# Input gradient of a convolution stem: the second batch with three products for all three leaves, each in its own PSUM tile

## The chip, the core and the metric

The kernel runs on one core of a Trainium2 chip. The metric is the device time of one execution in microseconds (us). The engines are TensorE (PE, matmuls, fed by weight loads, PEld), VectorE (DVE), ScalarE (ACT), GpSimd (POOL) and SyncE (SP, which issues nearly all transfers here). The program lists the operations once, each with its inputs, outputs and an estimated duration, and a planner writes out the order of every engine by hand before anything is emitted.

## The reference

A strided one-dimensional convolution (31 taps, stride 2, 256 channels in and out, two batches of 16000 steps), a normalization over time, and a gelu; the outputs are the forward result and the gradients of all four inputs in bf16.

```
B, T, D, K = 2, 16000, 256, 31
s = 2
L = (T - K) // s + 1                         # 7985
h = sum over i of x[:, i:i + s*L:s, :] @ w[i]
mu, var = mean and variance of h over l
h = (h - mu) / sqrt(var + 1e-5) * gn_gamma + gn_beta
out = gelu(h)                                # tanh form
out, grads of (x, w, gn_gamma, gn_beta) for grad_out
```

## The kernel before

**Stages.** F0 and F1 are the forward of batches 0 and 1 (to about 422 us), G0 and G1 the input gradient (about 422 to 862 us), W the weight gradient (to the end). The gelu of batch 0 and its derivative run beside F1, those of batch 1 beside the first chunks of the input gradient.

**A convolution by fewer products.** The 31 taps are split three times in two. The first two levels use three products in place of four: branches B, A, C (`ORDER`) for the first, leaves B, A, C for the second. For each pair the weights of the branch and leaf are differences or originals, held in `W2`. At the third level a leaf can be computed plainly (`g_leaf`, 16 matmuls) or by three products again: `g_three_b` (4 matmuls with weight differences from `W2D`, and a copy with the sign changed into the second half of the PSUM tile) and `g_three_ac` (8 matmuls with the sums from `GU`). The sums of the moving data come from VectorE: `first` makes the branch's planes (`GS`) from the element tile `ET`, `second` those of leaves A and C (`GL`), `third` the third level's (`GU`, `GUO`).

**The input gradient now.** `input_grad` goes over batches `b`, chunks `c` (four a batch), half chunks `pr` and, innermost, branches `br`. A unit is one half chunk and branch. It takes two of the four PSUM tiles (`slots4`): leaf B goes into `px` by three products, `g_seed` turns that and the kept results of branch B (`GRB`, fp32) into the starting values of leaves A and C on VectorE or ScalarE, and in the next unit `last(A)` and `last(C)` accumulate these leaves on top, and `g_evac` copies them into `HO`. In batch 0, A and C are plain; in batch 1 (`GO`) leaf A has three products, whose difference product `g_outer` lies in the other tile and is joined through `GTS` (fp32). After branch C's leaf C one transfer of 1 MB per half chunk writes `out_1`.

**What feeds it.** For each chunk `e_load` loads the stored gelu derivative (into `EG`) and h (into `EH`), `e_comp` scales and adds them into the gradient of the convolution's output and spreads it into one of two tiles `ET`; `dn_turn` transposes it and stores it to DRAM (`dn_d`). From there `d2_piece`, seven pieces a batch, computes the differences for the weight gradient (line 1338) and stores them to `d2_d`, from which `d_tile` of the weight gradient loads its tiles. The pieces share one source tile `DT`.

**The order.** `Plan.add` records an operation and what it must wait for; `due` times are worked back from the end over durations, with `lead` shifting a kind of operation; `listing` runs a list schedule. TensorE may take an operation up to `look` = 14 ahead of its written order. Operations on transfers get part of their slack added:

```
room = max(0.0, due[s] + slip - r) * 0.3
if ops[s]["dma"] is not None:
    r += min(self.pads[0 if o["dma"] is None else 1], room)
```

Lines the text names: 1168 matmuls of the input gradient, 602 of the forward, 1428 of the weight gradient; 682 and 686 joins of 1024 elements, 689 and 693 of 512; 697 copies out of PSUM, 1195 the sign copy; 1127 sums; 557 weight differences; 1073, 1075 and 1077 scaling and adding, 1087 spreading; 1338 the pieces; 1042 the last statistic of a batch; 1394, 1488, 1496, 1520 and 1566 work of the weight gradient on VectorE; 974 products of the gelu part; 1457 the emission of weight gradients; 424 and 429 transfers.

## Time and profile before

| | |
|---|---|
| time, median of 3 runs | 1189.31 us (1188.89 to 1189.55) |
| span of the profiled execution | 1190.2 us |
| TensorE busy | 1148.1 us, 96% |
| VectorE busy | 1044.0 us, 88% |
| ScalarE busy | 578.9 us, 49% |
| GpSimd busy | 24.9 us, 2% |
| transfers | 255.17 MB, mean 214 GB/s |
| granted TensorE clock | 0.997 |

Busy times are unions over an engine's instructions; the mean of a group counts each instruction from its start to its end, and neighbours overlap a little. A row of the waits gives what waited, for whom, the total, the number and the longest. A row by windows gives the window, its length, and for each engine the busy time and the number of instructions, then the granted clock, the busy share of the transfer engines and GB/s. The chain of waits is followed back from the last instruction.

### The profile page before, as it was taken

The page shows a single profiled execution, that of the slowest core. Times are in us where ns is not written, and L with a number is a line of the kernel's source. Part 1 is how long each engine was busy: PE and PEld are TensorE (multiplying, and loading weights), DVE is VectorE, ACT ScalarE, POOL GpSimd, SP SyncE. Part 2 cuts the span into 40 slices and gives each one's busy share as a digit, 9 for nine tenths or more (in the row PEclk, how much of TensorE's full clock was granted, in tenths as well). Part 3 has the DMA queues.
Part 4 walks back from the last instruction along what each step waited for, and adds up shares of the span by engine and source line. Part 5 has one row for each costly group of instructions (what it writes and reads, how often), then busy time and mean ns, then how long its engine had stood idle before and what let it go on. Part 6 is the DMA issues. An engine that isn't in the chain of part 4 may idle for free.

```text
span 1190.2 us, 19351 instructions
## 1 busy us (share of the span) xinstructions
PE 1148.1 (96%) x7755; PEld 764.2 (64%) x7812; DVE 1044.0 (88%) x1351; ACT 578.9 (49%) x879; POOL 24.9 (2%) x67
## 2 busy tenths in 40 slices
PE   5999999999999999999999999999998999989998
PEld 4888899776776964444444444444487766656685
DVE  7997798899999989999889897788888999679995
ACT  1244454678875578978785776433222212211200
POOL 0000000000000000101000000000000000000000
PEclk9999999999999999999999999999999999989999
DMA  9464838889894799766738998697898727997674
GB/s 212 67 140 103 184 92 194 197 186 196 195 231 109 252 318 268 214 221 161 236 123 260 287 321 286 167 312 251 281 258 270 236 91 229 327 306 237 226 215 116
DMA packets 334084, 255.17 MB, mean 214 GB/s; under 512 B 187484, under 2 KB 312666, under 8 KB 325722
## 3 DMA queue, kind: packets, MB, share of 16 engines
q1 hardware_dynamic: 333802, 253.93, 76.2%
q8 instruction: 61, 1.00, 0.3%
q14 instruction: 29, 0.24, 0.1%
q0 software_dynamic: 192, 0.00, 0.0%
HBM read 118.95 MB, written 89.62 MB: 175 GB/s over the span
## 4 chain that ended last, share of the span: by engine, by line
PE 72%; DVE 11%; DMA 7%; ACT 4%; issue 3%; SPq 2%; POOL 0%; DVEq 0%; ACTq 0%; POOLq 0%
PE ps L602 30%; PE ps L1168 24%; PE ps L1428 17%; DVE arena L1394 2%; DMA arena<-dnd 2%; DMA arena<-d2d 2%; DMA d2d<-arena 1%; DVE arena L1338 1%; DMA arena<-in_x_dram 1%; SPq L429 1%; ACT arena L717 1%; DVE arena L557 1%; DVE arena L1488 1%; DVE arena L1496 1%; SPq L424 1%
## 5 line engine op out<-in xcount | busy, mean ns | idle before, releaser
L1168 PE MATMUL ps<-arena 128*128 128x512 bf16 (+1 forms) x1974 | 429.2, 376 | 5.3 <-DVE ps L682 2.0
L602 PE MATMUL ps<-arena 128*128 128x256 bf16 (+4 forms) x3460 | 407.2, 280 | 21.6 <-DVE arena L557 7.5
L602 PEld LDWEIGHTS <-arena 128*128 128x128 bf16 x3460 | 337.1, 98 | 91.8 <-issue 8.8
L1168 PEld LDWEIGHTS <-arena 128*128 128x128 bf16 x2016 | 197.4, 98 | 235.8 <-issue 4.9
L1428 PE MATMUL ps<-arena 128*128 128x256 bf16 (+1 forms) x2321 | 312.6, 297 | 11.7 <-DVE arena L1488 5.4
L1428 PEld LDWEIGHTS <-arena 128*128 128x128 bf16 x2336 | 229.7, 98 | 94.6 <-issue 6.2
L697 ACT ACTIVATE arena<-ps 128x1024 f32<-128x1024 f32 (+1 forms) x143 | 145.9, 1021 | 250.4 <-PE ps L1428 95.0
L567 DVE TENSOR_TENSOR arena<-arena 128x1088 bf16<-128x1088 bf16 (+3 forms) x211 | 175.2, 865 | 15.4 <-PE ps L602 14.4
L974 DVE TENSOR_TENSOR arena<-arena 128x1024 bf16<-128x1024 bf16 x160 | 106.7, 683 | 10.1 <-ACT arena L966 6.4
L1127 DVE TENSOR_TENSOR arena<-arena 128x516 bf16<-128x516 bf16 (+3 forms) x176 | 83.7, 507 | 14.1 <-PE ps L1168 13.3
L1394 DVE TENSOR_TENSOR arena<-arena 128x4096 bf16<-128x4096 bf16 x38 | 86.1, 2282 | 3.6 <-DMA arena<-in_x_dram 1.8
L682 DVE TENSOR_TENSOR ps<-ps,arena 128x1024 f32<-128x1024 f32 x60 | 73.3, 1224 | 12.9 <-PE ps L1428 8.1
L1338 DVE TENSOR_TENSOR arena<-arena 128x768 bf16<-128x768 bf16 (+3 forms) x112 | 65.9, 636 | 10.1 <-DMA arena<-dnd 6.8
L717 ACT ACTIVATE arena<-ps 128x512 bf16<-128x512 f32 (+1 forms) x64 | 36.9, 580 | 59.7 <-PE ps L602 59.7
L682 DVE TENSOR_TENSOR ps<-arena,ps 128x1024 f32<-128x1024 f32 x44 | 53.8, 1223 | 9.5 <-PE ps L1168 5.3
L1512 ACT COPY ps<-ps 128x256 f32<-128x256 f32 x54 | 19.3, 358 | 81.1 <-PE ps L1428 79.9
L1496 DVE TENSOR_TENSOR arena<-arena 128x1024 bf16<-128x1024 bf16 x76 | 49.0, 682 | 8.2 <-DMA arena<-d2d 6.7
L1566 DVE TENSOR_TENSOR arena<-arena 128x2304 bf16<-128x2304 bf16 x36 | 47.8, 1349 | 4.1 <-DMA arena<-d2d 4.1
L1195 ACT ACTIVATE ps<-ps 128x512 f32<-128x512 f32 x48 | 27.9, 582 | 47.6 <-PE ps L1168 47.3
L557 DVE TENSOR_TENSOR arena<-arena 128x2048 bf16<-128x2048 bf16 (+1 forms) x52 | 50.5, 990 | 0.0
L672 ACT ACTIVATE arena<-ps 128x512 f32<-128x512 f32 x56 | 29.0, 601 | 38.9 <-PE ps L602 32.9
L638 ACT ACTIVATE ps<-ps 128x256 f32<-128x256 f32 x75 | 27.5, 367 | 41.0 <-PE ps L602 39.8
(79 smaller groups left out, 672.1 us busy)
## 6 DMA issues: line engine op xcount, KB each, us to landing
arena<-in_x_dram SPq DMA_DIRECT2D x40, 1024.0 KB, 9.4
arena<-d2d SPq DMA_DIRECT2D x16, 1216.0 KB, 10.5
out_dram<-arena SPq DMA_DIRECT2D x14, 1024.0 KB, 5.5
d2d<-arena SPq DMA_DIRECT2D x30, 384.0 KB, 7.3
arena<-dnd SPq DMA_DIRECT2D x10, 960.0 KB, 6.6
vl<-arena SPq DMA_DIRECT2D x36, 256.0 KB, 3.3
arena<-vl SPq DMA_DIRECT2D x9, 1024.0 KB, 5.6
hd<-arena SPq DMA_DIRECT2D x8, 1024.0 KB, 5.2
```

The costliest lines, as they stand in the source:

```text
L557: add("DVE", dve(n), [o], [a, b], lambda: nc.vector.tensor_tensor(out=o, in0=a, in1=b, op=ALU.subtract))
L567: lambda: nc.vector.tensor_tensor(out=o, in0=a, in1=b, op=ALU.add))
L602: yield nc.tensor.matmul(ps[:, dh, cs], lhsT=wt, rhs=mv, start=s0, stop=False, skip_group_check=True)
L682: add("DVE", dve(1024, 1), [out], [a, b], lambda: nc.vector.tensor_tensor(out=out, in0=a, in1=b, op=op))
L697: lambda: nc.scalar.activation(out=out, in_=ps, func=ACT.Copy, scale=scale))
L974: add("DVE", dve(1024), [o], [a, b_], lambda: V.tensor_tensor(out=o, in0=a, in1=b_, op=op))
L1127: lambda: nc.vector.tensor_tensor(out=o, in0=a, in1=b, op=ALU.add))
L1168: yield nc.tensor.matmul(ps[:, e, 0:wide], lhsT=lt, rhs=mv, start=s0, stop=False, skip_group_check=True)
L1338: lambda: nc.vector.tensor_tensor(out=out, in0=a, in1=b_, op=ALU.subtract))
L1394: add("DVE", dve(4096), [o], [a, b], lambda: nc.vector.tensor_tensor(out=o, in0=a, in1=b, op=ALU.add))
L1428: yield nc.tensor.matmul(ps[:, s, c0:c1], lhsT=lt, rhs=mv, start=s0, stop=False, skip_group_check=True)
L1496: add("DVE", dve(1024), [d4[:, j]], [d], lambda j=j, o=o, st_=st_: nc.vector.tensor_tensor(out=d4[:, j], in0=d[:, o:o + 3 * st_ + 1:st_, : ...
```

## The change

The units of batch 1 and of chunk (0, 3), named by `GV`, are computed by `split`: leaves B, A and C each by three products in a PSUM tile of its own, handed out by a list `free`. Leaf B is copied to SBUF in bf16 (`VT`), joined there with `GRB` (now bf16), and the finished leaves are joined with that in bf16 on the way to `HO`: by a copy and a join in place for all of branch B and for leaf A, by one join out of PSUM for leaf C of branches A and C (`GE`). The other units (`plain`) start leaves A and C from leaf B alone and join with `GRB` at the end. `W2D` holds nine differences in place of three and three in `W2DO`. The loop over branches lies outside that over the half chunks; `out_1` is written by `g_store` after each branch A and C, 512 KB in runs of 1024 bytes. There is one `ET` and one `GS` in place of two; the spreading is a step of its own, `e_spread`, placed after the first half of branch C of the chunk before. In the forward, the kept results `RB` and `TS` are bf16. The table `lead` is replaced, and some addresses of the weight gradient move.

```
-    RB = sb(146944, 2, 1024, dt=FP32)
+    RB = sb(146944, 2, 1024)
...
-    ET = [sb(o, 2, 4, 2, EM) for o in (165376, 182016)]
-    GS = [sb(o, 2, 2, 2, 2, EM) for o in (190336, 94336)]
+    EG, ET = sb(86016, 2, 2, 4, HM), sb(165376, 2, 4, 2, EM)
+    GS = sb(181888, 2, 2, 2, 2, EM)
...
-                ve(t, RB[:, j], t, ALU.add if br == A else ALU.subtract)
+                add("DVE", dve(1024), [t], [RB[:, j], t], lambda t=t, j=j: nc.vector.tensor_tensor(
+                    out=t, in0=RB[:, j], in1=t, op=ALU.add if br == A else ALU.subtract))
...
+    def g_join(o, a, b, op, rate):
+        add("DVE", dve(1024, rate), [o], [a, b], lambda: nc.vector.tensor_tensor(out=o, in0=a, in1=b, op=op))
+
+    def g_store(b, c, pr, br, ho):
+        n0 = 512 * c + 256 * pr
+        r = P if c < 3 or pr == 0 else 104
+        dst = bass.AP(tensor=out_1.tensor, offset=out_1.offset + (b * T + 8 * n0 + 2 * (br == C_)) * C,
+                      ap=[[16 * C, r], [4 * C, 4], [1, 2 * C]])
+        load(dst, ho[0:r].rearrange("p e k f -> p (e k) f"), r * 4096, 1024, "POOL", slack=60.0)
+
+    GV = {(b, c) for b in range(NB) for c in range(NCK) if (b, c) >= (0, 3)}
+    GE = {(b, c, pr, br, lf) ... if br == B_ or lf == A}
...
+        def plain(b, c, pr, br, o, sums):
...
+            g_three_b(px, br, B_, pl[B_], o)
+            if pr == 0:
+                second(A)
+            step()
+            g_three_ac(px, br, B_, gu[B_], o)
+            if pr == 0:
+                second(C_)
+            step()
+            keep(flat2(pt), flat2(px), -1.0)
...
+                g_leaf(ps, br, lf, pl[lf], o, False)
...
+                    g_join(ho[:, :, j, :], ps[:], rb, ALU.subtract if br == A else ALU.add, 1)
...
+        def split(b, c, pr, br, o, sums):
...
+            x = free.pop(0)
+            if pr == 0:
+                third(B_)
+            g_three_b(ring[x], br, B_, pl[B_], o)
+            if pr == 0:
+                second(A)
+            step()
+            a = free.pop(0)
+            g_three_b(ring[a], br, A, pl[A], o)
+            if pr == 0:
+                third(A)
+                second(C_)
+            g_three_ac(ring[x], br, B_, gu[B_], o)
+            vx = vtile()
+            keep(vx, ring[x][:])
+            free.append(x)
+            step()
...
+                g_join(ts[C_], vx, GRB[:, pr, 1], ALU.subtract if br == A else ALU.add, 2)
+                g_join(vx, vx, GRB[:, pr, 0], ALU.add if br == A else ALU.subtract, 2)
+            k = free.pop(0)
+            g_three_b(ring[k], br, C_, pl[C_], o)
+            if pr == 0:
+                third(C_)
...
+            last(A)
+            rest.append(lambda: last(C_))
...
+                for br in ORDER:
+                    sums = g_sums(br, k)
+                    k += 1
+                    sums[0]()
+                    for pr in range(2):
+                        (split if (b, c) in GV else plain)(b, c, pr, br, P * pr, sums)
...
+        if (br, pr) == (C_, 0) and nxt < (2, 0):
+            e_spread(*nxt)
```

473 lines of the change are left out of this document (244 added, 229 removed).

## The prediction

> **What bounds the kernel now.** I read the page first, then the busy time by stage, then the waits of TensorE in the input gradient, and last the chain of waits around the end of that stage. The profiled execution has this span; it stands 0.9 us above the median of the runs (1189.31), so I work on 1190.2 and take 0.9 off at the end.
>
> ```profile
> span 1190.2 us, 19351 instructions
> ```
>
> The busy times of three stretches: the end of the forward of the second batch, the input gradient (about 422 to 862 us), and the weight gradient.
>
> ```profile
> core 0: us, PE busy (x) PEld busy (x) DVE busy (x) ACT busy (x) POOL busy (x), PEclk, DMA share, GB/s
> 300.00:422.00 122.00, 120.28 (x977) 95.18 (x976) 118.33 (x166) 82.73 (x142) 3.81 (x11) 1.00 0.81 195
> 422.00:862.00 440.00, 434.78 (x2041) 203.55 (x2080) 385.42 (x608) 287.83 (x356) 16.86 (x43) 1.00 0.81 247
> 862.00:1190.00 328.00, 313.02 (x2324) 229.81 (x2337) 277.04 (x240) 54.95 (x89) 0.53 (x1) 0.99 0.74 229
> ```
>
> The reader is to see two nearly full engines. In the input gradient TensorE is busy 434.8 of 440 us; VectorE 385.4, which is 88%; ScalarE 287.8, which is 65%. What TensorE waits for in the whole stage is next to nothing; these are all its waits, in total, number and longest:
>
> ```profile
> PE ps L1168 <- DVE ps L682: 2.0, 3, 1.4
> PE ps L1168 <- ACT arena L697: 0.5, 1, 0.5
> PE ps L1168 <- ACT arena L717: 0.5, 1, 0.5
> ```
>
> So the stage is bound by TensorE, and matmuls taken away shorten it as long as nothing else comes to the front. One thing stands close behind. In the chain of waits for 780 to 870 us no matmul of the input gradient carries the time from 783 us to the weight gradient: the differences of the output gradient (d2_piece of batch 1) do, from a load of dnd through VectorE to a store into d2d and a load out of it. Where it leaves TensorE, its last steps, and TensorE at the same place:
>
> ```profile
> 779.75 3.20 PE ps L1168 x14
> ...
> 836.06 4.41 DMA arena<-dnd
> ...
> 848.79 10.15 DMA d2d<-arena
> 859.02 5.68 DMA arena<-d2d
> 864.74 5.29 PE ps L1428 x47
> ```
>
> ```profile
> 862.40 0.60 PE L1428 MATMUL ps<-arena 128*128 128x256 bf16 x4
> 864.74 31.60 PE L1428 MATMUL ps<-arena 128*128 128x256 bf16 x288 [1.74 <-DMA arena<-d2d]
> ```
>
> TensorE ended the input gradient at about 862.4, did four matmuls of batch 0, and then stood 1.74 us until the d2 tile of batch 1 was there. The two ends meet within about 2.3 us: whatever shortens the matmuls of the input gradient meets the d2 chain at once.
>
> **The matmuls.** The code fixes their number: three products a leaf cost 4 + 8 matmuls, a plain leaf 16. A unit (a half chunk and a branch) now has 12 + 16 + 16 = 44 in batch 0 and 4 + 4 + 8 + 8 + 16 = 40 in batch 1; a split unit has 3 x 12 = 36. All 24 units of batch 1 lose 4 and the 6 units of chunk (0, 3) lose 8: 96 + 48 = 144 matmuls out of 2016. The price of one comes from the busy times of line 1168 alone, by weight loads, since some matmul records are missing:
>
> ```profile
> 650.00:758.00 108.00, 107.47 (x496) 49.41 (x505) 1.00 0.93 281
> ```
>
> 108 us by 505 is 0.214 us, so the change removes 144 x 0.214 = 30.8 us. That this is saved at all hangs on what follows.
>
> **VectorE in the input gradient.** The prices, from the groups by shape:
>
> ```profile
> L974 DVE TENSOR_TENSOR arena<-arena 128x1024 bf16<-128x1024 bf16 x160 | 106.7, 683 | 10.1 <-ACT arena L966 6.4 <-ACT arena L968 2.6
> ...
> L682 DVE TENSOR_TENSOR ps<-ps,arena 128x1024 f32<-128x1024 f32 x60 | 73.3, 1224 | 12.9 <-PE ps L1428 8.1 <-ACT arena L697 4.8
> ...
> L1127 DVE TENSOR_TENSOR arena<-arena 128x514 bf16<-128x514 bf16 x68 | 28.2, 423 | 1.3 <-PE ps L1168 1.3
> ...
> L1457 DVE TENSOR_TENSOR arena<-ps,arena 128x1024 bf16<-128x1024 f32 x15 | 18.3, 1218 | 6.8 <-PE ps L1428 6.8
> ...
> L689 DVE TENSOR_TENSOR arena<-ps,arena 128x512 f32<-128x512 f32 x16 | 10.9, 683 | 2.8 <-PE ps L1168 1.4 <-ACT arena L697 1.2
> ```
>
> and, since an instruction's busy time overlaps its neighbour's in a dense run,
>
> ```profile
> 741.96 1.23 DVE L682 TENSOR_TENSOR ps<-arena,ps 128x1024 f32<-128x1024 f32 x1
> 743.09 1.22 DVE L1077 TENSOR_TENSOR arena<-arena 128x2048 bf16<-128x2048 bf16 x1
> ```
>
> the second starts 1.13 us after the first, so I take 0.09 off each. Added: the sums third for leaf C in 12 (chunk, branch) pairs and for A and C in three more, 18 pairs of 2 x 0.33 us = 11.9 us. The joins before, for a half chunk of batch 1: five of 1024 in fp32 on PSUM (1.13) and four of 512 (0.60), 8.05 us; eight halves are 64.4 us, and chunk (0, 3) has eight of 1.13, 9.0 us. After, for a half chunk: branch B two joins all in bf16, which I price by the 1024-wide bf16 instruction of line 974 (0.60), branches A and C each three of these and one from PSUM, priced by line 1457 (1.13): 1.2 + 2 x 2.93 = 7.06 us, ten halves 70.6. So the joins get 2.8 us cheaper. The weight differences for leaf C are three more instructions like these:
>
> ```profile
> L557 DVE TENSOR_TENSOR arena<-arena 128x2048 bf16<-128x2048 bf16 x30 | 36.0, 1215 | 0.0
> ```
>
> 3.4 us. Together +12.5: VectorE needs 398 us in a stage that shall last 440 - 30.8 = 409, which is 97%. The nearest row for such a density is the stretch 300 to 422 above: VectorE 118.3 of 122 (97%), TensorE idle 1.7 us, or 1.4%. For 409 us that is 5.8, against the 3.0 of waits above that the stage loses today: +2.8 us, with 0 and +12 as the ends (nothing lost; twice that row's share). In the plain units left in batch 0 the seeds on VectorE become joins from PSUM at the same price, so nothing changes there.
>
> **ScalarE and the PSUM ring.**
>
> ```profile
> L697 ACT ACTIVATE arena<-ps 128x1024 f32<-128x1024 f32 (+1 forms) x143 | 145.9, 1021 | 250.4 <-PE ps L1428 95.0
> ...
> L1195 ACT ACTIVATE ps<-ps 128x512 f32<-128x512 f32 x48 | 27.9, 582 | 47.6 <-PE ps L1168 47.3
> ```
>
> Per split half chunk ScalarE has nine copies of 0.58 and seven of 1.02, 12.4 us, against 9.0 now (five of about 0.58 and six of 1.02); in a plain half chunk branches A and C each have one of 1.02 less. That is +26 in batch 1, +7 in (0, 3), -12 in the plain chunks: 309 of 409 us, 76%. The sign copy behind each first product is covered by the 12 matmuls between it and its use (2.6 us), which a 0.58 copy behind one 1.02 copy fits into; a freed PSUM tile is written again 24 matmuls (5.1 us) after its last one. Nothing from me for this; if the cover is gone, 0.2 us for each of 30 units, 6 us. The output stores become 32 half-size transfers in place of 16, in shorter runs, all in SyncE's one queue, where the d2 stores also stand; that belongs to the next part.
>
> **The d2 chain.** It is the step that moves against the change. Today the element tile ET is doubled, so the gradient of chunk (1, 3) was computed while chunk (1, 1) still ran. With one ET and the copies in e_spread, the chain is: branch B of (1, 1) has read ET; e_spread (1, 2); then the gradient buffer EG is free for the load of (1, 3); scaling, adds, transposes, dnd, seven pieces. SyncE's queue and ScalarE today:
>
> ```profile
> 721.99 0.51 SPq L424 DMA_DIRECT2D arena<-dyd  x1
> ...
> 744.84 5.51 SPq L429 DMA_TRANSPOSE arena<-arena  x2
> ...
> 757.65 0.35 SPq L424 DMA_DIRECT2D arena<-dnd  x1
> ...
> 825.03 0.33 SPq L424 DMA_DIRECT2D arena<-dnd  x1
> ...
> 836.06 0.33 SPq L424 DMA_DIRECT2D arena<-dnd  x1
> ```
>
> ```profile
> 729.98 4.25 ACT L1075 ACTIVATE arena<-arena,stats 128x1024 bf16<-128x1024 bf16 x4
> ...
> 745.47 0.82 ACT L1087 COPY arena<-arena 128x768 bf16<-128x768 bf16 x1
> ...
> 747.10 3.34 ACT L1087 COPY arena<-arena 128x768 bf16<-128x768 bf16 x5
> ```
>
> With G ending at 862.4 - 30.8 - 1 + 2.8 = 833 and chunks of 216 x 0.214 = 46.2 us, chunk (1, 1) starts at 694.4. Branch B's second half has read ET after 40 matmuls, at 703; e_spread takes 5 us of copies (745.5 to 750.4 above) and some POOL copies, to 710; the load of dyd was followed by its first scaling 8.0 us later, four of those (4.25) and the last add make about 14 us, to 724; from the transposes to the first dnd load are 12.8 us (744.84 to 757.65), to 737; from there to the first matmul of batch 1 today's trace takes 864.74 - 757.65 = 107.1 us: 844. The pieces start 13.0 us apart on average (757.65 to 836.06, six steps), at best 11.0 (825.03 to 836.06), and the planner stretches DMA-bound steps where it sees slack; at the best pace the chain gains 6 x 2 + 2 = 14 us: 830. So TensorE would find its data between 830 and 844, when it is ready at 833 + 0.6. I take 840, nearer the traced pace because VectorE, which each piece needs for some 4 us, is fuller: a gap of about 7 us where there are 2.3 today, +4.7.
>
> Such a gap costs more than itself. The weight gradient has one already, 5.07 us up to 1044.7; the granted clock after it:
>
> ```profile
> 1040.00:1044.00 4.00, 0.00 (x0) 0.00 (x0) 4.00 (x5) 0.23 (x1) 0.00 (x0) 0.91 1.04 331
> ...
> 1048.00:1050.00 2.00, 2.00 (x12) 1.39 (x11) 0.00 (x0) 0.61 (x2) 0.00 (x0) 0.50 1.09 346
> 1050.00:1052.00 2.00, 2.00 (x19) 1.79 (x18) 0.00 (x0) 1.07 (x3) 0.00 (x0) 0.97 1.10 349
> ```
>
> The clock stood at 0.50 for about 6 us after that gap. Those 3 lost us are all that the mean of 0.99 over 862 to 1190 leaves room for, so the gap of 1.74 cost nothing of the kind; a 7 us gap costs 3 more. The Trainium skill (TensorE: Matmul & The Clock Gate, Part 1: The HAM clock gate) says that the array falls to half clock after an idle window of about 3.4 us; the trace agrees, with 1.74 us below it and 5.07 above. Without the gate the sum would end at 1165, with it at 1168.
>
> **The rest.** The forward: the 20 joins of this group go from fp32 to bf16, from 1.13 to 0.60 us, 10.6 us of VectorE; but what TensorE waits for most there once it has started is ScalarE:
>
> ```profile
> L682 DVE TENSOR_TENSOR arena<-arena 128x1024 f32<-128x1024 f32 x20 | 24.1, 1221 | 7.5 <-ACT arena L672 6.4 <-ACT arena L697 1.0
> ```
>
> ```profile
> PE ps L602 <- ACT arena L717: 6.8, 9, 1.4
> ```
>
> With the new order I take -1, between -5 and +4. The start of batch 1's first chunk hangs on the statistics of the second batch, which ended here:
>
> ```profile
> L1042 DVE SCALAR_TENSOR_TENSOR stats<-small x2: 149/155/161, 399.7 to 629.4; 128x2 f32<-128x2 f32 x2
> ```
>
> 629.4; scaling and adds on VectorE and 5 us of copies follow, by 640 or so as an estimate; chunk (1, 0) will start at 833 - 4 x 46.2 = 648. Nothing, or 5 us if the gelu units run later. The weight gradient is the same work at other addresses. One of its first x tiles lies in GS, which is now read for the last time 40 matmuls before the end of the input gradient in place of 60, 4.3 us later; that stays within the gap at the d2 chain, and costs up to 4 if the chain is early. Its order otherwise: within 3 us either way.
>
> Sum: -30.8 + 2.8 + 4.7 + 3 - 1 = -21.3; 1190.2 - 21.3 = 1168.9, less 0.9: 1168.
>
> **Rivals.** First, all hidden: the chain compresses to its best pace and is ready as the matmuls end, and VectorE's density costs nothing: -30.8 - 1, 1157.5. For it: the planner gives the most urgent step the engine first, and both VectorE and TensorE run at 97 to 99% side by side in 300 to 422. Against: SyncE's queue already waits on the pieces.
>
> Second, e_spread (1, 2) runs at its written place, at the head of branch C, 31 us into the chunk and not 9: the chain is 22 us later, ready at 852 to 866. The gap is 19 to 33 us, 16.7 to 30.7 more than now; with -30.8 + 2.8 - 1 + 3 the sum is -9.3 to +4.7: 1180 at the best pace, 1194 at today's.
>
> Third, slower: VectorE becomes the bound. Today it idles 440 - 385.4 = 54.6 us of the stage. If that is no slack but latency (its queue is in order and each wait on a ScalarE copy or a matmul holds all sums behind it), the idle stays, and the stage lasts 398 + 54.6 = 452.6, 12.6 longer than now: 1189.3 + 11.6 = 1201. It decides from 42 us of idle that cannot be used. Against: the stretch 300 to 422 has 3.7 us of idle in 122.
>
> That the matmuls don't go away is excluded by the code.
>
> **Chances.** 0.42 for the forecast (1161 to 1176), 0.26 for all hidden (1153 to 1161), 0.18 for the late spread (1180 to 1194), 0.12 for VectorE, 0.02 for anything else. The range 1155 to 1187 leaves out the lower edge of the first rival, the upper half of the second, and the third. A measurement tells 0.2%, about 2.4 us, from no change. Faster: 0.42 + 0.26 + 0.12 of the second = 0.80; same 0.04 and slower 0.02 of the second, with the third and the rest slower 0.16.
>
> **What would show it.** Weight loads on the three-product lines fall from 2016 to 1872; the input gradient of TensorE lasts about 412 us; VectorE is above 95% busy there. At the head of the weight gradient stands a wait for d2d of 3 to 10 us, followed by a few us of granted clock near 0.50. I am wrong if TensorE waits on VectorE by more than 12 us inside the input gradient (third rival), if the chunk (1, 0) waits for the gelu units, or if the gap at the head is absent (first) or above 15 us (second).

## The result and the profile after

The changed kernel takes 1185.87 us (median of 6 runs, 1184.77 to 1186.12) against 1188.9 (6 runs, 1188.02 to 1189.55); the ratio is 0.997, with a 95% interval of 0.9958 to 0.9981. So it is 3 us faster, where 21 were forecast. The lines of the changed kernel that the text names: 1217 matmuls of the input gradient, 1500 of the weight gradient; 750 copies of PSUM tiles (evictions, and the starting values in plain units), 1244 sign copies; 1181 sums, 1259 joins; 1126 and 1128 scalings, 1146 halo copies and 1155 copies of the spreading; 1410 differences for the weight gradient, 1560 sums of the weight gradient on VectorE; 1014 to 1028 steps of the gelu part, 1096 the last statistic of a batch. Of the page after, the span and TensorE's busy time, then of its waits those in the input gradient (waiter, releaser, total, number, longest), with one of ScalarE above them:

```profile
span 1184.1 us, 19217 instructions
...
PE 1120.7 (95%) x7615; PEld 751.0 (63%) x7668; DVE 1043.5 (88%) x1410; ACT 595.9 (50%) x919; POOL 38.7 (3%) x67
```

```profile
ACT arena L1155 <- POOL arena L1146: 9.1, 4, 5.3
PE ps L1217 <- DVE arena L1181: 9.0, 1, 9.0
...
PE ps L1217 <- ACT arena L750: 7.8, 5, 2.4
...
PE ps L1217 <- ACT ps L1244: 6.3, 5, 2.9
...
PE ps L1217 <- DVE arena L1259: 3.4, 3, 2.1
```

The matmuls went as computed: 1872 weight loads on line 1217 in place of 2016 on line 1168, and 27 us less of busy TensorE. But where TensorE waited 3.0 us in the input gradient, it now waits 26.9: behind VectorE's sums (1181) once for 9.0, behind ScalarE's copies (750, 1244) for 14.1, behind joins (1259) for 3.4. To see where, I count weight loads and so find the end of each chunk (264 loads for a plain chunk; 240 for one of batch 1 before, 216 for a split one after). All later chunk times are made in this way; an end is known to about 0.3 us.

| chunk | before ends | after ends | after minus before | by matmuls alone | lost in this chunk |
|---|---|---|---|---|---|
| (0,0) | 485.3 | 496.7 | +11.4 | 0 | 11.4 |
| (0,1) | 541.4 | 557.8 | +16.4 | 0 | 5.0 |
| (0,2) | 597.9 | 613.9 | +16.0 | 0 | -0.4 |
| (0,3) | 654.0 | 660.0 | +6.0 | -10.3 | 0.3 |
| (1,0) | 705.4 | 715.6 | +10.2 | -15.4 | 9.3 |
| (1,1) | 756.8 | 765.0 | +8.2 | -20.5 | 3.1 |
| (1,2) | 808.3 | 815.3 | +7.0 | -25.7 | 4.0 |
| (1,3) | 862.0 | 862.3 | +0.3 | -30.8 | -1.6 |

The column by matmuls alone is the number of saved matmuls so far by 0.214 us; the last column is what the difference grew by beyond it. By this count the 30.8 us were made and 31.1 lost again before the weight gradient began: 23.9 of these are waits (26.9 for 3.0), and I put most of the rest to a lower clock and to the start (the first matmul of the stage came at 429.5 for 428.1), as an estimate. The eight chunks of the kernel after, by windows (busy time and number for PE, PEld, DVE, ACT, POOL, then clock, transfer share, GB/s):

```profile
428.00:496.70 68.70, 58.98 (x271) 27.37 (x276) 59.24 (x99) 52.92 (x71) 1.17 (x5) 0.93 0.92 283
496.70:557.80 61.10, 56.60 (x262) 25.94 (x266) 55.64 (x82) 41.48 (x50) 9.57 (x8) 1.00 0.68 190
557.80:613.90 56.10, 55.84 (x260) 25.84 (x264) 50.38 (x80) 44.94 (x54) 3.21 (x12) 1.00 0.64 197
613.90:660.00 46.10, 45.84 (x212) 21.12 (x216) 44.83 (x89) 33.43 (x47) 2.58 (x4) 1.00 0.52 148
660.00:715.60 55.60, 48.09 (x214) 21.46 (x217) 49.47 (x86) 45.43 (x57) 10.65 (x4) 0.97 1.03 327
715.60:765.00 49.40, 46.36 (x214) 21.16 (x217) 42.77 (x83) 35.92 (x47) 2.83 (x9) 1.00 0.90 265
765.00:815.30 50.30, 47.68 (x212) 21.50 (x216) 42.05 (x72) 26.49 (x37) 1.18 (x3) 0.97 0.84 264
815.30:862.30 47.00, 46.06 (x213) 21.10 (x216) 44.29 (x74) 23.37 (x31) 0.00 (x0) 1.00 0.93 309
```

and two of the kernel before, (0,1) and (1,0):

```profile
485.30:541.40 56.10, 55.84 (x261) 25.82 (x265) 53.46 (x78) 44.87 (x55) 3.27 (x5) 1.00 0.69 198
...
654.00:705.40 51.40, 51.14 (x237) 23.51 (x241) 46.57 (x74) 35.44 (x40) 2.21 (x4) 1.00 0.97 307
```

Chunk (0,3) shows the change at its best: 46.1 us for 216 matmuls, 45.8 of it busy. In (0,0) TensorE is idle for 9.7 us at a mean clock of 0.93; in (0,1) GpSimd is busy 9.57 us where it was 3.27; in (1,0) TensorE is idle for 7.5 us, with the transfers at 1.03. VectorE is nowhere near full over the stage: 388.7 of 434.3 us, 89.5%. The head of the weight gradient, and its later gap, on TensorE:

```profile
862.67 0.60 PE L1500 MATMUL ps<-arena 128*128 128x256 bf16 x4
864.76 46.90 PE L1500 MATMUL ps<-arena 128*128 128x256 bf16 x428 [1.48 <-DVE arena L1560]
...
1040.04 20.14 PE L1500 MATMUL ps<-arena 128*128 128x256 bf16 x137 [3.07 <-DVE arena L1560]
```

```profile
1040.00:1044.00 4.00, 3.96 (x37) 3.54 (x38) 3.12 (x3) 1.73 (x5) 0.00 (x0) 1.00 1.01 326
```

TensorE stands for 1.48 us at the head, now behind sums on VectorE (1560), where it stood 1.74 for d2d. The gap further on is 3.07 us in place of 5.07, and the clock behind it stays at 1.00 (third number from the end) where it fell to 0.50 before. From the end of the input gradient to the end of the span it was 328.2 us (862.0 to 1190.2) and is 321.8 (862.3 to 1184.1): in these two traces the span's gain of 6.1 us is that of the weight gradient, whose work did not change. Half of it is the choice of the trace: every run's time is 1.7 to 1.9 us above its span, so the traced execution before took about 1192.0, 3 us above the median of its runs, and the traced one after 1185.9, its median.

### The profile page after: what moved, and what is told of

Read it like the earlier page. It is cut to its first block, busy times and chain, and to the rows that moved or that the text cites. A ratio compares the mean times of both kernels' runs of the same rounds, so it can differ in the third digit from the quotient of the medians.

```text
span 1184.1 us, 19217 instructions
## 1 busy us (share of the span) xinstructions
PE 1120.7 (95%) x7615; PEld 751.0 (63%) x7668; DVE 1043.5 (88%) x1410; ACT 595.9 (50%) x919; POOL 38.7 (3%) x67
## 4 chain that ended last, share of the span: by engine, by line
PE 73%; DVE 10%; DMA 7%; ACT 5%; issue 3%; SPq 1%; POOL 1%; DVEq 0%; POOLq 0%; ACTq 0%; another core or an unknown queue 0%
PE ps L655 34%; PE ps L1500 20%; PE ps L1217 19%; DVE arena L1466 2%; DMA arena<-dnd 2%; DMA d2d<-arena 2%; DVE arena L1410 1%; DMA arena<-in_x_dram 1%; DVE arena L1259 1%; DMA arena<-hd 1%; SPq L480 1%; POOL arena L1146 1%; DVE arena L1181 1%; DMA arena<-d2d 1%; DVE arena L1568 1%
## 5 line engine op out<-in xcount | busy, mean ns | idle before, releaser
L1217 PE MATMUL ps<-arena 128*128 128x512 bf16 (+1 forms) x1834 | 404.5, 380 | 28.9 <-DVE arena L1181 9.0
L655 PEld LDWEIGHTS <-arena 128*128 128x128 bf16 x3460 | 338.4, 99 | 90.8 <-DVE arena L610 8.8
L1217 PEld LDWEIGHTS <-arena 128*128 128x128 bf16 x1872 | 184.3, 99 | 248.8 <-issue 28.7
L1500 PEld LDWEIGHTS <-arena 128*128 128x128 bf16 x2336 | 228.3, 98 | 88.0 <-DVE arena L1560 5.7
L750 ACT ACTIVATE arena<-ps 128x1024 bf16<-128x1024 f32 (+1 forms) x129 | 130.8, 1020 | 216.8 <-PE ps L1500 94.5
L1028 DVE TENSOR_TENSOR arena<-arena 128x1024 bf16<-128x1024 bf16 x160 | 107.7, 686 | 10.6 <-ACT arena L1020 7.0
L1181 DVE TENSOR_TENSOR arena<-arena 128x516 bf16<-128x516 bf16 (+3 forms) x212 | 98.2, 495 | 5.3 <-PE ps L1217 2.9
L1244 ACT ACTIVATE ps<-ps 128x512 f32<-128x512 f32 x108 | 62.3, 583 | 38.7 <-PE ps L1217 38.7
L1259 DVE TENSOR_TENSOR arena<-arena 128x1024 bf16<-128x1024 bf16 x80 | 54.8, 686 | 7.1 <-ACT arena L750 6.8
L1259 DVE TENSOR_TENSOR arena<-ps,arena 128x1024 bf16<-128x1024 f32 x44 | 53.7, 1220 | 3.4 <-PE ps L1217 3.3
L610 DVE TENSOR_TENSOR arena<-arena 128x2048 bf16<-128x2048 bf16 (+1 forms) x55 | 53.6, 1005 | 0.0
L725 ACT ACTIVATE arena<-ps 128x512 bf16<-128x512 f32 x56 | 29.1, 601 | 46.9 <-PE ps L655 41.7
L1018 DVE SCALAR_TENSOR_TENSOR arena<-arena 128x1024 bf16<-128x1024 bf16 x32 | 39.0, 1221 | 13.1 <-ACT arena L1016 13.0
L1568 DVE TENSOR_TENSOR arena<-arena 128x1024 bf16<-128x1024 bf16 x76 | 48.5, 685 | 1.6 <-DMA arena<-d2d 1.6
```

What stands on the lines that cost most here:

```text
L655: yield nc.tensor.matmul(ps[:, dh, cs], lhsT=wt, rhs=mv, start=s0, stop=False, skip_group_check=True)
L750: lambda: nc.scalar.activation(out=out, in_=ps, func=ACT.Copy, scale=scale))
L1028: add("DVE", dve(1024), [o], [a, b_], lambda: V.tensor_tensor(out=o, in0=a, in1=b_, op=op))
L1181: lambda: nc.vector.tensor_tensor(out=o, in0=a, in1=b, op=ALU.add))
L1217: yield nc.tensor.matmul(ps[:, e, 0:wide], lhsT=lt, rhs=mv, start=s0, stop=False, skip_group_check=True)
L1244: lambda: nc.scalar.activation(out=ps[:, 1], in_=ps[:, 0], func=ACT.Copy, scale=-1.0))
```

## The experiments

A plan made anew moves everything; so in some runs the order of the changed kernel is kept, on every engine, and only what an instruction does or where it runs is altered ("order kept").

**The chain to the weight gradient.** e4 takes away the wait for batch 1's differences.

```
-            load(D2[b]..., d2_d[b][i1 * 3 + i2], 19 * 65536, 4096)
+            load(D2[b]..., d2_d[0][i1 * 3 + i2], 19 * 65536, 4096)
```

> The changed kernel, but the weight gradient loads batch 0's d2 tiles for both batches (so its results are not the reference's); batch 1's pieces are computed and stored as before, nothing waits for them. Theory D: TensorE, VectorE and the loads are freed of the chain, and the planner can give the engines to the input gradient; 4 us faster or more. Theories H and O: TensorE ends the input gradient at the same time, only the 1.5 us gap goes; within 2 us of 1185.9.

Measured: 1185.96 us, ratio to before 0.9991 (0.9976 to 1.0005), the time of the changed kernel or a little more. TensorE's stops in the input gradient are as they were, and it ended at 859.7. The chain did not hold this kernel.

**The halo copies: twice the same edit.** e1 puts the 24 small copies of `e_spread` (line 1146) on ScalarE and plans anew; e6 does it with the order kept.

```
-                add("POOL", 0.3, [o], [i], lambda: nc.gpsimd.tensor_copy(out=o, in_=i))
+ e1             add("ACT", act(o.free_size()), [o], [i], lambda: nc.scalar.copy(out=o, in_=i))
+ e6             add("POOL", 0.3, [o], [i], lambda: nc.scalar.copy(out=o, in_=i))
```

> The changed kernel with its 24 halo copies of e_spread (four a chunk, at most 12 columns) on ScalarE in place of GpSimd; nothing else. Theory H (the lost gain sits in ScalarE's queue, which waits for these copies before it can spread, with sign copies and PSUM copies behind it): GpSimd's 26.2 us of copies and ScalarE's 9.1 us of waits for them go, TensorE's waits on ScalarE in the input gradient (14.1 us) fall to about 5, and the time falls by 6 to 10 us, to 1176 to 1180. Theory D (the d2 chain sets the start of the weight gradient): TensorE's waits fall the same way, but a wait for d2d takes their place at about 862 us and the time stays within 2 us of 1185.9. Theory V (VectorE's density): no change, within 2 us.

> The order of all work stays as in the changed kernel; only the 24 copies of halo columns are issued on ScalarE in place of GpSimd. Theory A (these copies, up to 8.7 us long, hold the spread and ScalarE's queue behind it): the waits of ScalarE for GpSimd (9.1 us) vanish, the stops of TensorE behind ScalarE copies at the starts of chunks (7.8 + 6.3 us) fall by 4 to 7 us in all, and the time falls by 3 to 7 us, to 1179 to 1183. Rival B (it is the copies' own amount on ScalarE that holds TensorE): the 24 copies add 24 x 0.2 us there, and the time stays within 2 us of 1186.

e1 took 1189.31 us, ratio 1.0009 (0.9990 to 1.0028); e6 1181.46, ratio 0.9932 (0.9909 to 0.9955): 4.4 us less than the change, and faster than both kernels. The mechanism, in the kernel after on GpSimd, ScalarE and TensorE:

```profile
505.97 8.78 POOL L1146 COPY arena<-arena 128x12 bf16<-128x12 bf16 x4 [63.35 <-DVE arena L1181]
```

```profile
512.38 0.83 ACT L1155 COPY arena<-arena 128x768 bf16<-128x768 bf16 x1 [5.28 <-POOL arena L1146]
```

```profile
514.90 5.34 PE L1217 MATMUL ps<-arena 128*128 128x512 bf16 x23 [2.89 <-ACT ps L1244]
```

Four copies of 12 columns and less took 8.78 us on GpSimd. ScalarE, in order, stood 5.28 us before its spread, and the sign copy for which TensorE then waited 2.89 us stood behind that. In e6 no such wait is left, and chunk (0,1) takes 56.1 us, as before the change:

```profile
496.40:552.50 56.10, 56.10 (x266) 25.83 (x265) 55.84 (x82) 41.88 (x55) 0.79 (x4) 1.00 0.75 208
```

e1 had the same copies at the same price and lost the gain to another order (9.2 us at the head, 8.3 behind sign copies). So 8 us lie between two plans of the same work, which is why small terms below are read from runs with the order kept. Even there the start of the stage moves from trace to trace (the first matmul between 426.6 and 430.3), and with it the end of (0,0).

**The head of the input gradient.** The first sums that leaf B needs write `GU`'s tile at 162752, which overlaps the scratch `JK` of the last statistics (163328). In the profile after:

```profile
440.76 5.41 PE L1217 MATMUL ps<-arena 128*128 128x512 bf16 x15 [9.00 <-DVE arena L1181]
```

```profile
439.14 1.22 DVE L1018 SCALAR_TENSOR_TENSOR arena<-arena 128x1024 bf16<-128x1024 bf16 x1 [2.37 <-ACT arena L1016]
440.28 0.42 DVE L1181 TENSOR_TENSOR arena<-arena 128x516 bf16<-128x516 bf16 x1
```

```profile
434.32 1.28 ACT L961 ACT_TABLE_LOAD   x1
...
436.73 1.24 ACT L1014 ACTIVATE arena<-arena,stats 128x1024 bf16<-128x1024 bf16 x1 [0.82 <-DVE stats L966]
...
440.26 1.28 ACT L1020 ACT_TABLE_LOAD   x1
...
444.39 1.01 ACT L750 ACTIVATE ps<-ps 128x1024 f32<-128x1024 f32 x1 [0.69 <-PE ps L1217]
```

TensorE stands 9.00 us for a sum of 0.42 us (1181, at 440.28). ScalarE was done with the scratch at 434.3 (783), so the address itself holds the sum for the first part of that time only; the planner, bound to keep the sum behind the scratch, has put it further back. VectorE has it behind a gelu product (1018), which waits for ScalarE (1016), and that comes after the statistics' square root and its table load (961). ScalarE then has three more gelu steps and a second table load before the first copy for TensorE (750, at 444.39). Before, that order was the other way about, and TensorE ran on:

```profile
437.71 1.02 ACT L697 ACTIVATE arena<-ps 128x1024 f32<-128x1024 f32 x1 [0.78 <-remote]
438.63 1.23 ACT L960 ACTIVATE arena<-arena,stats 128x1024 bf16<-128x1024 bf16 x1
```

```profile
432.33 16.14 PE L1168 MATMUL ps<-arena 128*128 128x512 bf16 x74
```

e2 removes one entry of the table `lead`, e3 does so with e1's edit, and e5 exchanges the two sets of `GU`; all three plan anew.

```
- e2, e3     "G0 tt third": -14.0,
- e5         gl, gu = GL[k % 2], GU[k % 2]
+ e5         gl, gu = GL[k % 2], GU[(k + 1) % 2]
```

> The changed kernel without the one entry of the table that makes the sums third of G0 due 14 us later. Theory O (the 9.0 us gap at the first chunk is the written order of VectorE, with the sums behind a gelu operation that waits for ScalarE): the gap falls to under 2 us and the clock loss behind it goes; 9 to 12 us faster, 1174 to 1177. Theory D: the input gradient starts 9 us earlier, but its end is held by the d2 chain; under 3 us. If the sums were late because their inputs were (the statistics of batch 0 ended 16 us later than in the kernel before), the gap stays at 6 to 9 us and the time within 3 us.

> Both edits of the two runs before. H and O together: 15 to 22 us faster than the changed kernel, 1164 to 1171. Theory D: at most 3 us faster, with 10 us or more of waiting for d2d at the head of the weight gradient.

> The two sets of the buffer GU change places, so that the first sums third of leaf B go to an address that no tile of the forward's end holds; the order is planned anew. Theory A (the 9.0 us in which TensorE stands at the head of the input gradient come from GU lying on the scratch of the last statistics): the gap falls under 2 us, the granted clock in 422 to 600 goes from 0.97 to 0.99, and the time falls by 6 to 11 us, to 1175 to 1180. Rival B (VectorE would be late there anyway, because the statistics of batch 0 end at 415 in place of 400): the gap stays above 6 us and the time within 3 us of 1186.

e2 took 1203.73 us, ratio 1.0140 (1.0118 to 1.0161), with a gap of 12.5; e3 1204.2, ratio 1.0148 (1.0119 to 1.0178). Neither touched the address, and both lost in new plans, so they don't decide on theory O. e5 took 1229.99 us, ratio 1.0343 (1.0318 to 1.0369), but its head is as theory A has it:

```profile
429.02 40.10 PE L1217 MATMUL ps<-arena 128*128 128x512 bf16 x188 [0.40 <-ACT arena L770]
...
652.82 26.22 PE L1217 MATMUL ps<-arena 128*128 128x512 bf16 x108 [7.42 <-ACT arena L1155]
...
899.32 20.88 PE L1500 MATMUL ps<-arena 128*128 128x256 bf16 x168 [20.93 <-DMA arena<-d2d]
```

```profile
L1096 DVE SCALAR_TENSOR_TENSOR stats<-small x2: 150/155/160, 413.7 to 644.2; 128x2 f32<-128x2 f32 x2
```

Chunk (0,0) ends at 485.4, as before the change, at a clock of 1.00. The address is all that was edited, so the plan with the gap does hang on it. But TensorE, now early, reached chunk (1,0) at 644.8 and waited 7.42 us for its elements: the statistics of batch 1 (the later of the two of line 1096) came at 644.2, 9.8 us later than in the changed kernel (634.4). And its d2 chain was late, with spreads hardly later than in the changed kernel (the last by 781 us, against 775): the weight gradient waited 8.80 and 20.93 us for d2d. e8, e5's edit with e6's and e7's, took 1229.5 us, ratio 1.0338 (1.0314 to 1.0363), where the gains should have added up to 1165 to 1174: the new plan of e5 outweighs the rest.

Five runs then tried to have the early head with the rest of the order kept. e9 moves the two sums ahead of the statistics (all of `GU` exchanged); e13 exchanges the B tiles alone, and also puts the first two copies (750; `kp`) with the matmuls that they read (`pe`) before the first and behind the second gelu step (`ge`); e17 puts all work but the gelu units and statistics 10 us earlier in the order, on top of e6's edit and an exchange of the B tiles; e10 and e14 are e9 and e13 with e6's edit. In e9 to e12 the exchanged tiles of A and C lie on sums `U` that the end of the forward still reads, so part of the forward computes with other numbers, by the same instructions.

```
+ e9    seq = [j for i in seq if i not in t3[2:4] for j in ([i] + t3[2:4] if i == t3[1] else [i])]
+ e13   seq = [x.get(i, i) for i in seq]                  # the pairs t3[0:2] and t3[2:4] change places
+ e13   seq = [j for i in seq if i not in mv for j in (pe[0:2] + kp[0:1] + [i] if i == ge[0]
+                 else [i] + pe[2:4] + kp[1:2] if i == ge[1] else [i])]
+ e17   return [1, 6, 14, ...]                           # the order, written out as a list
```

> The order of all work stays as in the changed kernel, but for two of VectorE's sums (leaf B's third sums of the first half chunk), which move ahead of the last statistics and the first gelu operation of batch 1; for that the two sets of GU change places. Theory A (these two sums, tied to the statistics by the buffer they share with their scratch, cost the 9.0 us at the head of the input gradient and the lower clock behind it): the gap falls under 2 us, the clock of 422 to 600 goes from 0.97 to 0.99 or 1.00, and 9 to 12 us are kept to the end: 1174 to 1177. Rival B (the order behind the head is tied to ScalarE's gelu work, so that what is won at the head is lost by the start of the weight gradient): the gap goes, and the time is 1182 to 1186.

> Both edits in the same fixed order: the two sums early, and the halo copies on ScalarE. Theory A (two separate stops): the gains add, 1169 to 1173, which is faster than both kernels. Rival B (they share their gain, since the work of ScalarE and VectorE between 440 and 515 us sets the pace of both): 1176 to 1181.

> The order of the changed kernel with one place altered by hand: leaf B's third sums of the first unit go to the other B tile of GU (exchanged for B alone) and into the place of the second unit's, ahead of the last statistics, and the first two sign copies of plain units (ScalarE, line 750) stand ahead of the first and after the second gelu operation in place of behind six of them. Theory A (the gap at the head is an order that holds on two queues: the sums behind the statistics on VectorE, the copies behind gelu on ScalarE): TensorE's stops between 428 and 446 us fall from 9.4 to under 3 us, the clock of 422 to 600 rises to 0.99, and the time falls by 6 to 10 us, to 1176 to 1180. Rival B (the start of the input gradient is slack, since what follows is bound by the next chunks' elements): the stops at the head go, and others of the same size come by 680 us; 1184 to 1187.

> e13_head_keep and e6_halo_fix together. Theory A: the gains add up, 1171 to 1176. Rival B: only that of the halo copies is left, 1180 to 1183.

> e6_halo_fix (halo copies on ScalarE) with the two B tiles of GU exchanged and one order on every queue: all work of the input gradient and after it that does not belong to the gelu units and statistics of batch 1 stands 10 us earlier in the planned order than those, as if TensorE had never stopped at the head; TensorE's own order is the same. In e13_head_keep the gap of 9 us hopped to the next thing that stood behind a gelu unit. Theory A (the gap is an order in which the gelu units are 9 us ahead of TensorE on both in-order queues): with the whole order shifted the stops between 428 and 460 fall under 3 us, chunk (1, 0) begins by 648 to 652 in place of 655, and the time falls by 4 to 9 us against e6_halo_fix, to 1173 to 1178. Rival B (the gelu units of batch 1 need their time on ScalarE and VectorE until 629 us, and what TensorE wins ahead of that it gives back at chunk (1, 0), as in e5_gu_swap, where it waited 7.4 us there for the elements): the stops move to 645 to 660 and the time stays at 1180 to 1184.

| run | time | ratio to before, 95% interval |
|---|---|---|
| e9_head | 1187.61 | 0.9996 (0.9982 to 1.0009) |
| e10_head_halo | 1184.43 | 0.9971 (0.9957 to 0.9985) |
| e13_head_keep | 1186.83 | 0.9988 (0.9976 to 1.0000) |
| e14_head_halo | 1182.09 | 0.9946 (0.9929 to 0.9962) |
| e17_shift | 1203.46 | 1.0115 (1.0098 to 1.0132) |

TensorE's stops in e9 and in e13:

```profile
433.99 5.31 PE L1217 MATMUL ps<-arena 128*128 128x512 bf16 x16 [3.50 <-DVE arena L1181]
444.11 67.47 PE L1217 MATMUL ps<-arena 128*128 128x512 bf16 x302 [4.80 <-ACT ps L750]
```

```profile
451.08 60.57 PE L1217 MATMUL ps<-arena 128*128 128x512 bf16 x276 [7.95 <-ACT arena L750]
```

The gap moved each time to the next thing for TensorE that stood behind a gelu step: in e9 half of it to the copy (750), in e13 nearly all to the next eviction, 1.44 and 7.95 us in place of 9.00. In e17, where the gelu units stand later beside all else, batch 1's statistics came at 652.5 and TensorE waited 7.99 us at 655, in chunk (0, 3), and 6.21 at the head. My expectation A was wrong in all five; for e14 rival B came (only the halo copies' gain was left). In e9, e13 and e17 chunk (0,0) ended no earlier for it (496.3, 496.4 and 498.5, for 496.7), so they never had the 9 us. Only the plan of e5 (and e8) had them, and gave 7.4 back at the start of (1,0), whose elements hang on the gelu units on the same two engines, and more in (1,1) by its new plan (60.7 us for 49.3). So the 9 us are a place in the order; whether an order exists that keeps them stays open. The halo copies gained 3.2 us here too (e10 against e9) and 4.7 (e14 against e13).

**ScalarE at the chunk starts.** Three prices, and the way round by VectorE: e11 cuts the sign copies on top of e10, e15 the scalings of batch 1 on top of e6, e7 moves these scalings (there are 24, not the 16 of the expectation) to VectorE, e12 moves them later in the order on top of e10.

```
+ e11   nc.scalar.activation(out=ps[:, 1, 0:64], in_=ps[:, 0, 0:64], func=ACT.Copy, scale=-1.0)
+ e15   nc.scalar.activation(out=hh[:, 0:128], in_=hh[:, 0:128], ...)      # and eh
+ e7    nc.vector.tensor_scalar(out=hh, in0=hh, scalar1=s5, scalar2=s6, ...)   # and eh
+ e12   for k, i in enumerate(scalings): self.start[i] += 2.0 + 1.5 * (k % 4)
```

> Order as in the changed kernel; the scaling of the elements of batch 1 goes from ScalarE (16 of about 1.05 us) to VectorE, which is 88 to 92% busy in the input gradient. Theory A (ScalarE's bursts of four scalings in front of sign copies stop TensorE): the stops behind ScalarE after 600 us (about 7 us) fall by 3 to 5 us, time 1181 to 1183. Rival B (VectorE is as tight as ScalarE): as much is lost behind VectorE, time 1185 to 1192.

> The run before with the sign copies of the input gradient cut from 512 columns to 64; the other 448 columns are left out, so this is a price and not a result. Some 78 copies of 0.58 us become about 0.2 us, 30 us less of ScalarE, with the number of its instructions and all waits as they were. Theory A (ScalarE's amount at the starts of chunks is what stops TensorE: the term that I put at nothing): TensorE's waits for ScalarE after 600 us (about 9 us) fall by more than half, and the time falls by 4 to 8 us against the run before. Rival B (the stops come from a few long bursts of scaling, and from transfers that ScalarE waits for at its head): the waits stay, and the time falls by less than 2 us.

> Both edits of e10_head_halo, and the 24 scalings of batch 1 on ScalarE moved later in the order by 2 to 6.5 us, so that sign copies and evictions come to stand between them; the amount of work is the same. Theory A (it is the burst, four scalings in a row behind a wait for their transfer, that holds the copies for TensorE): the stops after 600 us fall by 3 to 5 us, 1165 to 1169 if e10_head_halo is at 1170. Rival B (ScalarE's amount): the stops stay, within 1.5 us of e10_head_halo. Rival C (the gradient of the next chunk is late and with it the chain to the weight gradient): up to 6 us slower than e10_head_halo, with a longer wait for d2d at the head of the weight gradient.

> e6_halo_fix with the 24 scalings of batch 1 on ScalarE cut from 1024 columns to 128; the scaling of the other 896 is left out, so this is a price. A burst of four takes about 1 us in place of 4.3 to 4.6; the order and every wait stay. Theory A (the bursts hold sign copies and evictions, and the adds and spreads of the next chunk): the stops of TensorE between 660 and 680 and between 730 and 745 us, 9 us in e6_halo_fix, fall under 3 us, and the time by 5 to 9 us. Rival B (ScalarE waits at its head for the transfers of hd and dyd, and the copies stand behind that): half of the stops stay, and the time falls by less than 3 us.

e11: 1186.34 us, ratio 0.9977 (0.9965 to 0.9988), against 0.9971 for e10: ScalarE is busy 272.7 us from 422 to 862 in place of 312.5, and these 40 us (108 copies, not the 78 of the expectation) bought nothing: rival B. e15: 1181.31 us, ratio 0.9932 (0.9908 to 0.9956), the same as e6; the stops of 1.45 and 3.22 became 2.97 and a new one of 3.34 behind a join, and chunk (1,0) took 57.0 us against 55.0. Of the 9.1 us of stops that the expectation names, 6.0 stayed: rival B. e7: 1194.9 us, ratio 1.0045 (1.0032 to 1.0058): after 600 us the stops behind ScalarE fell from 9.9 to 4.6, as theory A has it, and those behind joins rose from 3.4 to 13.1: rival B, and dearer than it said. e12: 1197.41 us, ratio 1.0076 (1.0060 to 1.0093): nearly all that the input gradient lost against e10 (10.5 us) lies in (1,0) and (1,1), whose next elements hang on these scalings. So the amount of sign copies is not the price, and the length of the scalings alone is not either; no forecast of theory A on the time came true. What e15's traces show in place of the scalings stands below.

**Chunk (1,0).** TensorE in its first half after, and the clock over it (third number from the end):

```profile
675.34 1.02 PE L1217 MATMUL ps<-arena 128*128 128x512 bf16 x4 [2.39 <-ACT arena L750]
677.71 21.75 PE L1217 MATMUL ps<-arena 128*128 128x512 bf16 x94 [1.35 <-ACT arena L750]
```

```profile
672.00:674.00 2.00, 0.95 (x5) 0.32 (x4) 2.00 (x5) 2.00 (x3) 0.00 (x0) 1.00 0.70 238
...
676.00:678.00 2.00, 0.65 (x3) 0.19 (x2) 0.64 (x2) 2.00 (x4) 0.00 (x0) 0.74 1.02 330
678.00:680.00 2.00, 2.00 (x6) 0.74 (x5) 2.00 (x5) 2.00 (x4) 0.00 (x0) 0.50 1.07 262
```

No stop is longer than 2.39 us, but these two left TensorE 2.26 us of work in 6 (0.95, 0.66 and 0.65 in three windows of 2 us, of which the middle one is not shown), and the clock stood at 0.50 behind that. ScalarE in e6 at the same place:

```profile
657.15 4.26 ACT L1128 ACTIVATE arena<-arena,stats 128x1024 bf16<-128x1024 bf16 x4 [1.92 <-DMA arena<-dyd]
...
665.13 4.64 ACT L1126 ACTIVATE arena<-arena,stats 128x1024 bf16<-128x1024 bf16 x4 [1.24 <-DMA arena<-hd]
669.67 0.82 ACT L1155 COPY arena<-arena 128x768 bf16<-128x768 bf16 x1
```

It waits for dyd and for hd at its head, scales four times behind each, and then spreads, all within 22 us. e18 takes transfers away that run at the same time: the stores of batch 0's differences cut to 16 of 128 rows, on top of e6.

```
+            lambda: e.dma_start(out=out[0:rows] if rows else out, in_=...)     # rows = 16 for d2_d[0]
```

> e6_halo_fix with the stores of batch 0's differences to d2d cut to 16 of their 128 rows, in the same order (the rest of them is left out, and the weight gradient reads x in their place, as many bytes). In e6_halo_fix chunk (1, 0) lasts 55.0 us from 654.8 on, against 46.2 for its 216 matmuls, with the DMA engines at a mean share of 1.02 and three stops of TensorE by 676 us (1.45, 3.22, 1.35) followed by 4 us of clock near 0.50. Theory A (the transfers: the stores of d2 delay dyd and hd of the next chunk, ScalarE waits for these at its head and starts its scaling late, and the copies and the spread stand behind it): the chunk lasts 46 to 50 us and the time falls by 4 to 8 us, to 1174 to 1178. Rival B (ScalarE's order by itself: spread, scaling and copies fall into the same 20 us whenever the transfers land): 53 to 56 us, and the time within 2 us of e6_halo_fix.

```profile
664.66 4.63 ACT L1126 ACTIVATE arena<-arena,stats 128x1024 bf16<-128x1024 bf16 x4
```

e18 took 1178.08 us, ratio 0.9902 (0.9885 to 0.9918), 3.4 us less than e6, with intervals that overlap a little; chunk (1,0) took 52.6 us in place of 55.0 (54.9 to 57.0 in the other runs with the order kept and the scalings in place), which lies short of both theories. The stops are still there, shorter (1.86 for 3.22), and the clock stays at 1.00. By this one trace the stores are a part, some 2.4 us of 9.

Read beside it, e15's trace says why shorter scalings bought nothing:

```profile
662.99 1.65 ACT L1126 ACTIVATE arena<-arena,stats 128x128 bf16<-128x128 bf16 x4 [3.50 <-DMA arena<-hd]
```

```profile
692.28 1.09 DVE L1410 TENSOR_TENSOR arena<-arena 128x1792 bf16<-128x1792 bf16 x1 [3.80 <-DMA arena<-dnd]
```

With scalings of 1.65 us in place of 4.64 ScalarE only waited longer for hd (3.50 for 1.24), which came 10.3 us into the chunk in both (at 665.1 and 663.0, in chunks that began at 654.8 and 652.7); in e18 hd no longer held it, and the four scalings took their 4.63. The new stop of 3.34 in e15 is a join that stood on VectorE behind a difference waiting 3.80 for dnd, a transfer again. So hd and the scalings stand one behind the other in front of the same evictions, and each run shortened only one of them; no run has both.

**The split by itself.** e16 computes every chunk in the plain form.

```
-    GV = {(b, c) for b in range(NB) for c in range(NCK) if (b, c) >= (0, 3)}
+    GV = set()
```

> The changed kernel with no unit in three products for all leaves: every chunk of the input gradient in the form with three products for leaf B alone, 24 x 2 half chunks of 44 matmuls, 2112 in place of 1872, planned anew with the same table. Theory A (the new form as such, with one element tile and the loop over branches outside, is worth what the old one was): 240 x 0.214 = 51 us more for TensorE but none of the stops behind the three sign copies: 1215 to 1230. Rival B (the three products bring nothing here, since ScalarE and VectorE are the bound): 1186 to 1200.

1230.9 us, ratio 1.0362 (1.0328 to 1.0396). That is theory A, 0.9 us above its range. Against the changed kernel the 240 matmuls are worth 45 us, of 51.4 by their busy time; both numbers hold only as far as two plans can be compared (8 us above). But by the same price the kernel before, with 96 matmuls fewer than e16, would take 1188.9 + 20.5 = 1209 us with as many, so the new form (one element tile, branch loop outside, and its plan, made with a table for another kernel) is some 21 us dearer than the old one. Chunk (1,0) of e16 took 63.5 us for 264 matmuls, 7.0 too many, with no sign copy for leaves A and C in it: a loss of this size comes without the split too, there with a wait of 2.88 us for hd in front of the same four scalings.

## Why the prediction was wrong, point by point

**The matmuls** were right in number and price: 30.8 us ((0,3) took 46.1 us where I had 46.2).

**"ScalarE and the PSUM ring ... Nothing from me for this"** is the step that failed, with what I left out beside it: the start of the stage, and the copies on GpSimd, which stand in my text as "some POOL copies". I gave the losses in the stage 2.8 us; they were 31.1: 11.4 in (0,0), 5.0 in (0,1), 9.3 in (1,0), 3.1 and 4.0 in the next two, less 1.7 elsewhere. I had priced the cover by amounts: 12 matmuls, 2.6 us, against a 0.58 copy behind a 1.02 one. The amount itself I had right (309.2 us measured from 422 to 862 us, for 309), and it was harmless (e11). What stands ahead of a copy in ScalarE's queue is not one eviction but four scalings behind a transfer (1,0), a spread behind GpSimd (0,1), or five gelu steps and a table load (0,0). That TensorE waits behind these the traces show. Taking away the one behind GpSimd shortened the kernel (e6); the one of the head went away in e5, in a plan that lost more elsewhere. The bound that I wrote down, 6 us, came from the same picture of copies alone and was too small.

**VectorE at 97%** did not come about: the stage did not shrink, so VectorE is busy 89.5% of it, and TensorE waited for its joins 3.4 us. The added work was 9.3 us (388.7 against 379.4 from 428 on) for the 12.5 that I had. By its letter the sign of the third rival came (TensorE waited 12.4 us for VectorE), but 9.0 of that is one place in the order.

**The d2 chain**, +4.7 and +3 for the clock, was worth nothing here: TensorE came no earlier than before, and no wait for d2d was left at the head. e4 shows it for this kernel; what the chain does when TensorE comes at 833 no run shows, except that another plan makes it 30 us late (e5), and hardly by the late spread that my second rival had for it. That 1185.9 lies inside my range of 1155 to 1187 is luck: that part of it was kept for the late spread.

**The start of (1,0).** I put the statistics at 629 and the chunk at 648 and saw no conflict. In the changed kernel there is none (634.4 and 660.0). In e5, which has the early head, there is one of 7.4 us.

**The forward**, -1, can't be told: the input gradient began 1.4 us later than before (429.5 for 428.1), and this start moves by 3.7 us between runs of the same order. **The 0.9** that I took off at the end set a span against a time; the traced execution took about 1192.0, so 2.7 was to be taken off.

**The clock gate** was right at the head: nothing is lost after 1.48 us. It appeared where I had not looked, in (0,0), (1,0) and (1,2). In the weight gradient 3.07 us kept 1.00 where 5.07 had cost 3 us, but that was chance (last section).

**The weight gradient**, "within 3 us either way", gave 6.4 in the two traces, 3 by the clock and 2 by the shorter gap. I had no reason for it, and part of it is luck: with the same order it took from 320.9 us (e6) to 325.5 (e14), and the trace before is a slow one. Without it these two traces would be equally long.

**What stays open** is the larger part of the loss in (1,0) to (1,2). The amount of sign copies (e11) and the length of the scalings alone (e15) are excluded, and e16 has a like loss without the split. The d2 stores (e18) are about a quarter of the loss in (1,0), by one trace. Left are the late hd and the scalings together, which no run took away at once, and the one element tile, whose copies must run between the last read of one chunk and the first sum of the next. That is argued and not shown: a second tile wasn't tried.

## What to carry to other kernels

Price a change at each stage start and on each in-order queue, by what stands ahead of the new instruction there, not by whether the engine's total has room: here an engine at 70% cost more than 14 us, and cutting 40 us of its work gave nothing back. An address is an edge in the plan: one tile of 2 KB laid on another's scratch led to a stop of 9 us. When cutting one wait buys nothing, see what the engine waits for in its place before calling it harmless (e15). Test with the order kept, since the same edit planned anew came out 8 us apart, and count the ends of equal portions of work, which shows at once in which of them a gain is lost.

## What the runs showed of the hardware

A GpSimd copy of 12 columns and less took from 0.18 to 8.67 us beside VectorE: here the same 24 copies in the changed kernel and on ScalarE in e6 (nanoseconds: shortest, median, longest):

```profile
L1146 POOL COPY arena<-arena x24: 181/351/8673, 433.7 to 763.4; 128x12 bf16<-128x12 bf16 x12, 128x4 bf16<-128x4 bf16 x6, 128x2 bf16<-128x2 bf16 x6
```

```profile
L1146 ACT COPY arena<-arena x24: 177/191/206, 433.6 to 765.2; 128x12 bf16<-128x12 bf16 x12, 128x4 bf16<-128x4 bf16 x6, 128x2 bf16<-128x2 bf16 x6
```

The longest, 8.67 us, lay beside VectorE's additions and differences of two bf16 tiles each, one behind the other, and ended 0.14 us after VectorE had come to a join that reads one of its inputs from PSUM:

```profile
703.29 8.67 POOL L1146 COPY arena<-arena 128x12 bf16<-128x12 bf16 x1 [41.57 <-DVE arena L1181]
```

```profile
711.82 1.22 DVE L1259 TENSOR_TENSOR arena<-ps,arena 128x1024 bf16<-128x1024 f32 x1
```

The Trainium skill (SBUF — State Buffer, Who interferes with whom) says that a VectorE instruction with two inputs in SBUF contends with a GpSimd instruction that reads SBUF, and calls what they share an exclusive lock; the trace agrees, with 8.67 us on one side and 0.18 to 0.21 on ScalarE on the other.

The clock can fall without a long gap: after two stops of 2.39 and 1.35 us in chunk (1,0), with 2.26 us of work in 6, it stood at 0.50; with 2.79 us of work in 6 (668 to 674 us of e18) it stayed at 1.00. And the length of a single stop does not decide it. The same stop of the weight gradient kept 1.00 at 2.81, 2.93, 3.07 and 3.20 us (e6, e10, the changed kernel, e15) and was followed by some 3 us at 0.50 at 2.96, 3.22 and 3.31 us (e14, e11, e9). In e14:

```profile
1037.13 23.11 PE L1500 MATMUL ps<-arena 128*128 128x256 bf16 x144 [2.96 <-DVE arena L1560]
```

```profile
1038.00:1041.00 3.00, 3.00 (x16) 2.14 (x15) 2.21 (x2) 1.07 (x3) 0.00 (x0) 0.50 1.02 332
```

The Trainium skill (TensorE: Matmul & The Clock Gate, Part 1: The HAM clock gate) speaks of an idle window of about 3.4 us; these runs differ, since stops shorter than that lowered the clock.
